# A transformer block on one core: gate and up columns split over the two banks of a couple

## The chip, the cores and the metric

The kernel runs on one core of one Trainium2 chip. The metric is the device time of one launch in microseconds (us), as the median of several runs; smaller is better. The engines are called here as the profile calls them: PE (TensorE, with PEld for its weight loads), DVE (VectorE), ACT (ScalarE), POOL (GpSimd) and SP (SyncE, which issues the DMAs).

## What is computed

One block with 2048 rows of 512 columns: a conditioned layer norm, attention with 32 query heads of 16 columns that share one key and one value head, and a gated feed-forward part of 1792 columns. What the change touches is the last one:

```python
h = _layernorm(x) * (1 + cb) + sb            # 2048 x 512
g = jnp.einsum("bsd,df->bsf", h, w_gate)     # 512 x 1792
u = jnp.einsum("bsd,df->bsf", h, w_up)       # 512 x 1792
h = _sigmoid(g) * u
out = jnp.einsum("bsf,fd->bsd", h, w_down)   # 1792 x 512
x = x + gb * out
```

## The kernel before

The 2048 rows are taken in 8 blocks of 256 rows (QU), each of two row tiles of 128 (t = 0, 1). Attention runs in 32 units (block, group of 8 heads) of 16 steps. A step has four tiles of scores `st` (ACT takes the exponent into `P`), four tiles `sa` of the unit two ahead, of which DVE takes the row maxima (`mx`), and the products of `P` and `V` into the bank `craw`. Every one of these tiles is 128 x 512 in one PSUM bank and is made by four matmuls of 64 rows by 32 columns of the array (the helper `columns`, line 141); two such row halves run side by side. `sa` has three banks, `st` two, `craw` one.

The feed-forward part of block b runs in pieces between the attention work of block b + 1, at most one piece after each half step (`piece`). It is cut in `Couple`s: two accumulation groups of 12 terms (four tiles of K times three products of high and low halves in fp16), each in its own bank `pgu` (tag "b", two banks). A couple runs 24 places; at each place the two row halves of the array work for different groups, and after 12 places they change over. At the end of a couple both groups' `end` is called, which issues what empties the two banks (the eviction). Which piece comes after which half step is set by a planner (`pick`, `pace`, `parts`) that knows the number of places, not their time. PE, DVE, ACT and SP keep the program's order; only the last part (block 7, "the tail", after the loop) is put in order by a scheduler.

Before the change, a couple of gate and up (`gu_group`, line 884) has 256 gate columns and the 256 up columns of the same place in one bank, row tile 0 in the first bank and row tile 1 in the second. Its eviction is, for the first bank, a tanh of the gate half and a copy of the up half, both on ACT, and for the second bank a copy of the up half on DVE and a tanh of the gate half on ACT. When both row tiles are done, `gated_rows` (POOL) multiplies them and two DMA transposes turn them (`turned`) for the product with `w_down`. There are seven such couples in a block, one for each 256 columns, and seven blocks in the loop: 49 evictions. In the tail, groups of columns (`gu_cols`, line 926) run with full 128 x 128 weights instead.

The gate and up weights are split into high and low halves once, by POOL, stored to DRAM (`wD`) and loaded again for each block. A tile `gw` holds all of K for 256 columns (1 MB), and there are two of them (GWB). At the beginning of a couple `ask` puts four loads of 256 KB for the next tile on a list, from which `drip` issues one at each half step behind the transposes; `fetched` issues what is left when a couple needs it.

Of the kernel before, what the change touches and what calls it, by code (L numbers as in the profile page):

```python
# [8 lines left out]
F16 = mybir.dt.float16  # L9
F32 = mybir.dt.float32  # L10
AF = mybir.ActivationFunctionType
# [5 lines left out]
P = 128  # L17
# [7 lines left out]
QU = 256  # L25
NQ = S // QU
NKB = S // P
NDC = D // P
# [3 lines left out]
SH = 4.0  # L32
SW = 16.0
# [51 lines left out]

PBUFS = 4
SBANKS = {"st": 2, "sa": 3}
GWB = 2
HBUFS = 18
ABUFS = 6  # L90
NCH = F // 256


@with_exitstack
def adaln_mqa_glu_kernel(
# [29 lines left out]
    dr = ctx.enter_context(tc.tile_pool(name="dr", bufs=1, space=DRAM))  # L125
# [69 lines left out]

    class Couple:
        def __init__(self, a, c):
            self.gs, self.stage, self.w, self.n = (a, c), a.stage, a.w, 2 * a.n

        def part(self, n0, n1):  # L200
            if n0 == 0:
                for g in self.gs:
                    g.open()
            m = self.gs[0].n
            for n in range(n0, n1):
                if n == m:
                    assert self.since is not None or done[0] > self.marks
                    take_over(self.since)
                for j in (1 - side[0], side[0]):
                    g = self.gs[j ^ (n >= m)]  # L210
                    l_, r_, *cut = g.term(n % m, slice(64 * j, 64 * j + 64))
                    columns(cut[0](g.bank) if cut else g.bank, l_, r_, n == 0, n == 2 * m - 1)
                if n == m - 1:
                    self.since, self.marks = None, done[0]
                    if open_[0]:
                        hand_over()
                        self.since = done[0]
            if n1 == self.n:
                for k, g in enumerate(self.gs):
                    g.end(g.bank, k == 1)  # L220
# [5 lines left out]
    def t32(name, shape=(P, 512)):  # L226
        return wp.tile(list(shape), F32, tag="f32", name=name, bufs=18)
# [27 lines left out]
    sp1 = Ordered(nc.sync)  # L255
# [74 lines left out]
    def split_weight(src, hi, lo, shape, then=None):  # L330
        w_ = t32("wst", [P] + shape)
        sp1.dma_start(w_, src)

        def split():
            pool.tensor_scalar(w_, w_, SW, 0.0, op0=ALU.mult, op1=ALU.add)  # L335
            pool.tensor_scalar(hi, w_, 1.0, 0.0, op0=ALU.mult, op1=ALU.add)
            pool.tensor_tensor(lo, w_, hi, op=ALU.subtract)
            if then is not None:
                defer(WSTORE, then)

        defer(WLATE, split)
# [417 lines left out]
        waits.append((now[0] + n, f_))  # L759

    WO = {}
    wD = dr.tile([NCH, P, NDC, 4, 256], F16, name="wD")
    CH = [*range(2, NCH), 0, 1]
    FS = [2 * c_ + e for c_ in CH for e in range(2)]

    def gw_tile():
        return P2.tile([P, NDC, 4, 256], F16, tag="gw", name="gw", bufs=GWB)

    def weight_jobs():
        jobs = []
        gw = {}

        def gate_up(c_, m, kk):
            if (m, kk) == (0, 0):
                gw[c_] = gw_tile()
            ks = slice(2 * kk, 2 * kk + 2)
            split_weight((w_gate, w_up)[m][2 * kk * P:2 * (kk + 1) * P, c_ * 256:(c_ + 1) * 256].rearrange("(k p) n -> p k n", p=P),
                         gw[c_][:, ks, m], gw[c_][:, ks, 2 + m], [2, 256],  # L780
                         (lambda: sp1.dma_start(wD[c_], gw.pop(c_))) if (m, kk) == (1, 1) else None)
# [3 lines left out]
        for c_ in CH:  # L785
            for m in range(2):
                for kk in range(2):
                    jobs.append(lambda c_=c_, m=m, kk=kk: gate_up(c_, m, kk))
# [9 lines left out]
    use, gws = [0], {}  # L798
# [9 lines left out]
    def fetched(upto):  # L808
        while loads and loads[0][0] <= upto:
            loads.pop(0)[1]()  # L810

    def ask(upto):
        while use[0] <= upto:
            k = use[0]
            gws[k] = gw = gw_tile()
            for z in range(NDC):
                loads.append((k, lambda gw=gw, k=k, z=z: sp1.dma_start(gw[:, z], wD[CH[k % NCH], :, z])))
            use[0] += 1

    def ffn_block(b, end_of_all=False):  # L820
        x1, xrs, h2, ups, ths, gT = {}, {}, {}, {}, {}, {}
        at = b * NCH
        HF = 6

        def wo_group(t):
# [55 lines left out]

            return t_, go

        def gu_group(c_, t):
            def begin():
                if t == 0:
                    fetched(at + c_)
                    ask(at + c_ + 1)
                    ths[c_], ups[c_] = t32("th"), t32("u")

            def term(n, rs):
                k, i = divmod(n, 3)
                gw = gws[at + c_]
                h_, w_ = ((0, 0), (1, 0), (0, 1))[i]
                return h2[t][0][rs, 4 * h_ + k, :], gw[rs, k, 2 * w_:2 * w_ + 2, :].rearrange("p m n -> p (m n)")

            def end(p_, second):
                ts = slice(256 * t, 256 * (t + 1))
                th, u_ = ths[c_], ups[c_]
                if second:  # L900
                    dve.tensor_copy(u_[:, ts], p_[:, 256:])
                    act.activation(th[:, ts], p_[:, :256], AF.Tanh, scale=0.5 / (SH * SW))
                else:
                    act.activation(th[:, ts], p_[:, :256], AF.Tanh, scale=0.5 / (SH * SW))
                    act.activation(u_[:, ts], p_[:, 256:], AF.Identity)
                if t == 1:
                    gated_rows(c_)

            return Group("gu", 12, "pgu", term, end, begin)

        def gated_rows(c_):
            th, u_ = ths.pop(c_), ups.pop(c_)
# [5 lines left out]
            gT[c_], go = turned(rows, f"g{c_}")  # L918
            if not tail:
                defer(GLATE, go)  # L920
                return
            go()
            while turns:
                drip()

        def gu_cols(c_, m):
            def begin():
                if m == 0:
                    ask(at + c_ + 1 if c_ < NCH - 1 else at + c_)
                    fetched(at + c_ + 1)  # L930

            def term(n, rs):
                e, (k, i) = n // 12, divmod(n % 12, 3)
                gw = gws[at + c_]
                h_, w_ = ((0, 0), (1, 0), (0, 1))[i]
                return gw[rs, k, 2 * w_ + m, e * P:(e + 1) * P], h2[k][rs, h_, :QU], lambda z: z[:, e * QU:(e + 1) * QU]

            def end(p_, second):
                if m == 0:
                    ths[c_] = th = t32("th")  # L940
                    act.activation(th, p_, AF.Tanh, scale=0.5 / (SH * SW))
# [4 lines left out]
                pool.tensor_tensor(g_[:, 1], th, g_[:, 0], op=ALU.subtract)  # L946
                gT[c_] = g_

            return Group("gu", 24, "pgu", term, end, begin)

        def g_of(h_, f, t, rs):
            c_, e = divmod(f, 2)
            if end_of_all:
                return gT[c_][rs, h_, e * QU + t * P:e * QU + (t + 1) * P]
            return gT[c_][rs, 4 * h_ + 2 * t + e, :]

        def down_group(t, lo):
            n_ = HF if lo == 0 else NFC - HF
# [37 lines left out]
        downs = [[down_group(t, lo) for t in range(2)] for lo in (0, HF)]  # L996
        if end_of_all:
            return wos, turn_rows, [[gu_cols(c_, m) for m in range(2)] for c_ in range(NCH)], downs
        gs = [Couple(gu_group(c_, 0), gu_group(c_, 1)) for c_ in range(NCH)]
        for g in gs:  # L1000
            g.needs = [(b, "h20"), (b, "h21")]
        for ds in downs:
            gs.append(Couple(*ds))
            gs[-1].needs = [(b, f"g{c_}") for c_ in (range(HF // 2) if len(gs) == NCH + 1 else range(NCH))]
        first = Couple(*wos)
        for g in [first, *gs]:
            g.b = b
# [249 lines left out]
```

## Time and profile before

| what | value |
|---|---|
| median of three runs | 1642.88 us (1642.43 to 1643.03) |
| the profiled execution: its own time | 1645.27 us |
| the profiled execution: span from first to last instruction | 1643.5 us, mean clock 0.991 |
| busy in the span | PE 1600.6, DVE 1415.8, ACT 1303.2, POOL 666.3 us |
| loop with feed-forward pieces | about 350 to 1550 us of the span |
| tail (block 7) | about 1553 to 1643 us |

The profiled execution is 2.39 us over the median. Busy time of PE is the union of its matmuls from start to modelled end, so that a wait shorter than the matmuls still in flight does not show as idle time; the timeline's starts show it. A row of the timeline gives the start in us, the length in us, the engine, the line, the operation and the tile, and how many were merged.

### The profile page before, as it was taken

How to read it: one execution, taken by the hardware profiler on the slowest of the kernel's cores; microseconds unless marked ns; L12 is line 12 of the kernel's file. 1: busy time of each engine (PE TensorE's matmuls, PEld its weight loads, DVE VectorE, ACT ScalarE, POOL GpSimd, SP SyncE). 2: the span in 40 equal slices, each digit the busy share in tenths (PEclk: the TensorE clock that was granted, in tenths of full speed). 3: DMA queues.
4: the chain of work that ended last, by engine and by line, in shares of the span. 5: the costliest groups of instructions: out<-in, count | busy, mean ns of one | idle time of the engine just before them, and what ended most of it. 6: DMA issues, size and time to landing. Idle time of an engine off the chain costs nothing.

```text
span 1643.5 us, 91921 instructions
## 1 busy us (share of the span) xinstructions
PE 1600.6 (97%) x41481; PEld 982.2 (60%) x41481; DVE 1415.8 (86%) x2400; ACT 1303.2 (79%) x2409; POOL 666.3 (41%) x827
## 2 busy tenths in 40 slices
PE   6899999999999999999999999999999999999998
PEld 3335444556666666666666566666666666665465
DVE  7789999999899999999999999999999999993041
ACT  5539989888888888888888888888888888888600
POOL 5453777244326232443226232543226322532222
PEclk9979999999999999999999999999999999999999
DMA  7121454136421433134412433134312432134522
GB/s 240 67 83 64 150 167 130 28 84 131 99 48 33 107 82 83 29 90 102 91 38 56 91 96 67 31 86 103 91 36 67 105 86 67 22 95 96 115 74 81
DMA packets 171301, 140.22 MB, mean 85 GB/s; under 512 B 96036, under 2 KB 129820, under 8 KB 170012
## 3 DMA queue, kind: packets, MB, share of 16 engines
q1 hardware_dynamic: 170908, 134.34, 32.0%
q8 instruction: 325, 5.32, 1.4%
q14 instruction: 68, 0.56, 0.1%
HBM read 97.18 MB, written 16.24 MB: 69 GB/s over the span
## 4 chain that ended last, share of the span: by engine, by line
PE 89%; DVE 3%; ACT 3%; DMA 2%; issue 1%; SPq 1%; POOL 0%; POOLq 0%; ACTq 0%
PE craw L141 25%; PE pgu L141 18%; PE sa L141 18%; PE st L141 11%; PE pd L141 8%; PE po L141 2%; PE pq L141 2%; PE pd L192 2%; PE pgu L192 2%; DVE mx L141 2%; ACT P L141 1%; DMA xall<-in_A_x_dram 1%; SPq L141 1%; ACT th L141 1%; DVE st L141 0%
## 5 line engine op out<-in xcount | busy, mean ns | idle before, releaser
L141 DVE TENSOR_REDUCE mx<-sa 128x1 f32<-128x512 f32 x2048 | 1309.7, 684 | 87.7 <-PE sa L141 38.5
L141 ACT ACTIVATE P<-st 128x512 f32<-128x512 f32 x2048 | 1180.7, 599 | 204.6 <-PE st L141 141.5
L141 PE MATMUL craw<-P,V 64*32 64x512 f32 x8192 | 1090.3, 597 | 2.0 <-issue 1.0
L141 PE MATMUL st<-qp,kp 64*32 64x512 f16 x8192 | 836.4, 379 | 6.4 <-ACT P L141 5.3
L141 PE MATMUL sa<-kp,qp 64*32 64x512 f16 (+1 forms) x7940 | 831.6, 378 | 7.1 <-DVE mx L141 5.5
L141 PEld LDWEIGHTS <-kp 64*32 64x32 f16 x8192 | 326.1, 91 | 262.6 <-issue 92.6
L141 PE MATMUL pgu<-gw,h 64*32 64x512 f16 x9408 | 422.2, 376 | 6.4 <-issue 3.6
L141 PEld LDWEIGHTS <-qp 64*32 64x32 f16 (+1 forms) x7940 | 269.5, 92 | 138.3 <-issue 52.2
L141 PEld LDWEIGHTS <-h 64*32 64x32 f16 (+1 forms) x9600 | 211.3, 92 | 90.5 <-issue 36.3
L141 PEld LDWEIGHTS craw<-P,V 64*32 64x32 f32 x8192 | 190.3, 105 | 24.7 <-issue 5.8
L141 PE MATMUL pd<-wdh,g 64*32 64x512 f16 x2688 | 136.6, 376 | 0.7
L913 POOL TENSOR_SCALAR th<-th 128x512 f32<-128x512 f32 x49 | 30.3, 618 | 242.2 <-ACT th L141 158.8
L565 POOL MEMSET qp<- 32x1024 f16 x60 | 56.6, 944 | 131.9 <-PE st L141 129.6
L141 PEld LDWEIGHTS <-g 64*32 64x32 f16 x4032 | 82.0, 92 | 30.8 <-issue 6.3
L721 POOL TENSOR_TENSOR raw<-raw 128x256 f32<-128x256 f32 x31 | 22.7, 732 | 164.7 <-DMA raw<-lD 142.3
L141 PE MATMUL pd<-wdl,g 64*32 64x512 f16 x1344 | 81.0, 376 | 0.0
L914 POOL TENSOR_TENSOR th<-th,u 128x512 f32<-128x512 f32 x49 | 62.8, 1282 | 4.1
L969 POOL TENSOR_TENSOR ot<-ot,gb 128x512 f32<-128x512 f32 x12 | 15.3, 1279 | 114.3 <-ACT ot L141 114.3
L917 POOL TENSOR_TENSOR gr<-th,gr 128x512 f16<-128x512 f32 x49 | 57.1, 1165 | 4.1
L141 PE MATMUL craw<-nought 64*32 64x1 f16 x357 | 58.2, 163 | 0.0
L141 PE MATMUL pq<-h,wdh 64*32 64x512 f16 (+1 forms) x688 | 54.8, 390 | 0.5 <-DVE h L141 0.4
L335 POOL TENSOR_SCALAR wst<-wst 128x512 f32<-128x512 f32 x46 | 28.4, 618 | 53.6 <-DMA wst<-in_B_w_down_dram 26.7
(156 smaller groups left out, 1131.3 us busy)
## 6 DMA issues: line engine op xcount, KB each, us to landing
gw<-wD SPq DMA_DIRECT2D x224, 256.0 KB
wD<-gw SPq DMA_DIRECT2D x7, 1024.0 KB
wm<-in_w_mod_dram SPq DMA_DIRECT2D x6, 1024.0 KB
qp<-qD SPq DMA_DIRECT2D x192, 32.0 KB
qD<-q SPq DMA_DIRECT2D x16, 256.0 KB
xr<-in_A_x_dram SPq DMA_DIRECT2D x16, 256.0 KB
out_dram<-ot SPq DMA_DIRECT2D x16, 256.0 KB
raw<-cs SPq DMA_DIRECT2D x248, 16.0 KB
```

Of the source, the lines that this page charges most:

```text
L141: return (lambda *a, **k: keep(f_(*a, **k))) if pinned else f_
L192: pe.matmul(cut[0](self.bank) if cut else self.bank, l_, r_, start=(n == 0), stop=(n == self.n - 1))
L335: pool.tensor_scalar(w_, w_, SW, 0.0, op0=ALU.mult, op1=ALU.add)
L565: eng.memset(qp[j:j + 32], 0.0)
L721: keep(pool.tensor_tensor(raw[:, :QU], raw[:, :QU], raw[:, QU:], op=ALU.mult))
L913: pool.tensor_scalar(th, th, 1.0, 1.0, op0=ALU.add, op1=ALU.mult)
L914: pool.tensor_tensor(th, th, u_, op=ALU.mult)
L917: pool.tensor_tensor(rows[:, 1], th, rows[:, 0], op=ALU.subtract)
L969: pool.tensor_tensor(ot, ot, mods[5], op=ALU.mult)
```

## The change

A couple now takes one row tile: 512 gate columns in one bank and the 512 up columns in the other (`gu_pair`). Three pairs of 512 columns and two row tiles make six couples; the remaining 256 columns stay as they were (`gu_last`), so that a block still has seven couples of the same number of places. The eviction of a pair is one tanh of 512 columns on ACT and one copy of 512 columns on DVE. The weights are kept by rows of K: a tile `gw` is [128, 4, 512] (512 KB: gate high, up high, gate low, up low for one tile of K), seven of them form the ring, and a block uses 14. A tile's slot is asked for again as soon as its last term in the second couple of a pair has been issued (`after`), in two loads of 256 KB; so a block still has 28 loads. The stores to DRAM are 28 of 256 KB with runs of 512 bytes for the pairs, in place of 7 of 1024 KB. The names of the turned tiles and the terms of the product with `w_down` follow.

```diff
-GWB = 2
+GWB = 7
+NPR = NCH // 2
+NGW = 4 * NPR + 2
...
-    wD = dr.tile([NCH, P, NDC, 4, 256], F16, name="wD")
+    wD = dr.tile([NPR, NDC, P, 4, 512], F16, name="wD")
+    wD1 = dr.tile([2, P, 2, 4, 256], F16, name="wD1")
...
+            def store():
+                for k in range(2):
+                    dst = wD[i // 2, 2 * kk + k, :, :, i % 2 * 256:(i % 2 + 1) * 256] if i < 2 * NPR else wD1[kk, :, k]
+                    sp1.dma_start(dst, g_[:, k])
...
+    def ask(spent):
+        while use[0] < min(spent + GWB, NGW * NQ):
...
+        def gu_pair(p, t, m):
+            def begin():
+                if m == 0:
+                    fetched(at + NDC * (p + 1) - 1)
+            def term(n, rs):
+                k, i = divmod(n, 3)
+                h_, w_ = ((0, 0), (1, 0), (0, 1))[i]
+                return h2[t][0][rs, 4 * h_ + k, :], gws[at + NDC * p + k][rs, 2 * w_ + m]
+            def end(p_, second):
+                if m == 0:
+                    ths[p, t] = th = t32("th")
+                    act.activation(th, p_, AF.Tanh, scale=0.5 / (SH * SW))
+                    return
+                u_ = t32("u")
+                dve.tensor_copy(u_, p_)
+                gated_rows(ths.pop((p, t)), u_, f"g{p}{t}")
...
-        gs = [Couple(gu_group(c_, 0), gu_group(c_, 1)) for c_ in range(NCH)]
+        gs = [Couple(gu_pair(p, t, 0), gu_pair(p, t, 1)) for p in range(NPR) for t in range(2)]
+        for p in range(NPR):
+            for k in range(NDC):
+                gs[2 * p + 1].after[12 + 3 * k + 2] = lambda spent=at + NDC * p + k + 1: ask(spent)
+        gs.append(Couple(gu_last(0), gu_last(1)))
```

The order of PE's instructions in the loop is the same, matmul for matmul, except for the names of the tiles and what the first matmul of a bank waits for. ACT's order at the first eviction (`th` and `u` are the eviction, `P` is attention), before:

```order
L141 ACTIVATE P_8815<-st 128x512
L141 ACTIVATE th<-pgu 128x256
L141 ACTIVATE u<-pgu 128x256
L141 ACTIVATE th<-pgu 128x256
L141 ACTIVATE P_8844<-st 128x512
```

and after:

```order
L143 ACTIVATE P_8836<-st 128x512
L143 ACTIVATE th<-pgu 128x512
L143 ACTIVATE P_8882<-st 128x512
L143 ACTIVATE cs<-craw 128x512
L143 ACTIVATE P_8900<-st 128x512
```

Three instructions stand between two exponents before, one of twice the width after. On DVE the copy keeps its place among the maxima and changes its width alone, 128x256 to 128x512. PE at the beginning of the second couple, where the two banks of the first are taken again (`h_...` are the turned rows of a row tile), before:

```order
L141 MATMUL st_8974<-qp_6718,kp_135 32x512
L141 LDWEIGHTS h20_7744 [waits DMAHW0_49,PE_49]
L141 MATMUL pgu_8983<-gw_8428,h20_7744 32x512 [waits Activation_49]
...
L141 LDWEIGHTS h21_7839
L141 MATMUL pgu_8984<-gw_8428,h21_7839 32x512 [waits Activation_49]
```

and after:

```order
L143 MATMUL st_9012<-qp_6747,kp_135 32x512
L143 LDWEIGHTS h21_7874 [waits DMAHW3_49]
L143 MATMUL pgu_9018<-gw_7774,h21_7874 32x512 [waits Activation_49]
...
L143 LDWEIGHTS h21_7874
L143 MATMUL pgu_9019<-gw_7774,h21_7874 32x512 [waits DVE_49]
```

Before, both banks wait for ACT; after, the first waits for ACT and the second for DVE. In the tail, PE between the last use of the first `gw` slot that is loaded again and the first use of its new content, before (28 matmuls between the two):

```order
L192 MATMUL pgu_50416<-h2c_50381,gw_49676 128x256
...
L192 LDWEIGHTS gw_50445 [waits DMAHW4_49]
L192 MATMUL pgu_50511<-h2c_50367,gw_50445 128x256
...
L192 LDWEIGHTS gw_50445 [waits DMAHW5_49]
```

and after (37 between the two):

```order
L194 MATMUL pgu_50477<-h2c_50377,gw_48869 128x256
...
L194 LDWEIGHTS gw_50506 [waits DMAHW7_49]
L194 MATMUL pgu_50518<-h2c_50391,gw_50506 128x256
...
L194 LDWEIGHTS gw_50506 [waits DMAHW0_49]
```

The scheduler has put more matmuls between release and use than stood there before.

More of the change, by code (lines that the diff above doesn't have):

```diff
@@ L197, in __init__ @@
         def __init__(self, a, c):
-            self.gs, self.stage, self.w, self.n = (a, c), a.stage, a.w, 2 * a.n
+            self.gs, self.stage, self.w, self.n, self.after = (a, c), a.stage, a.w, 2 * a.n, {}
         def part(self, n0, n1):
@@ L217, in part @@
                         self.since = done[0]
+                if n in self.after:
+                    self.after[n]()
             if n1 == self.n:
@@ L810, in fetched, with weights @@
             loads.pop(0)[1]()
[L812 to L817, printed above, removed]
-            use[0] += 1
+    def ask(spent):
+        while use[0] < min(spent + GWB, NGW * NQ):
+            u = use[0]
+            gws[u] = gw = gw_tile()
+            i = u % NGW
+            src = wD[i // NDC, i % NDC] if i < NDC * NPR else wD1[i - NDC * NPR].rearrange("p k m n -> p (k m n)").rearrange("p (m n) -> p m n", n=512)
+            for z in range(2):
+                loads.append((u, lambda gw=gw, src=src, z=z: sp1.dma_start(gw[:, 2 * z:2 * z + 2], src[:, 2 * z:2 * z + 2])))
+            use[0] += 1
+    def weights(b, i, k, w_, m):
+        at = b * NGW
+        if i < 2 * NPR:
+            return gws[at + NDC * (i // 2) + k][:, 2 * w_ + m, i % 2 * 256:(i % 2 + 1) * 256]
+        return gws[at + NDC * NPR + k // 2].rearrange("p m n -> p (m n)").rearrange("p (k m n) -> p k m n", k=2, m=4)[:, k % 2, 2 * w_ + m]
     def ffn_block(b, end_of_all=False):
         x1, xrs, h2, ups, ths, gT = {}, {}, {}, {}, {}, {}
-        at = b * NCH
+        at = b * NGW
         HF = 6
```

63 lines of the change are left out of this document (34 added, 29 removed).

## The prediction

> **What bounds the kernel now.** I read the page first (busy time by engine), then the table by stages for the loop, then the groups of instructions, then the list of waits, and at last the timeline around single evictions.
>
> ```profile
> PE 1600.6 (97%) x41481; PEld 982.2 (60%) x41481; DVE 1415.8 (86%) x2400; ACT 1303.2 (79%) x2409; POOL 666.3 (41%) x827
> 500.00:700.00 200.00, 198.53 (x5890) 131.78 (x5882) 189.42 (x318) 172.91 (x321) 82.11 (x97) 1.00 0.29 69
> ```
>
> The second row is a stretch of the loop; after the bounds and the length come PE, PEld, DVE, ACT and POOL busy, the granted clock, the DMA share and GB/s. PE is busy for 99% of it at full clock, DVE for 95%, ACT for 86%. So PE's order sets the pace, DVE follows closely, and the 1% of idle PE looks as if nothing could be won at the banks. The list of waits says the same: for the banks of gate and up that ACT empties it has 0.6 us, for the `sa` banks that DVE empties 5.5 us.
>
> ```profile
> PE sa L141 <- DVE mx L141: 5.5, 13, 1.4
> ...
> PE pgu L141 <- ACT u L141: 0.6, 4, 0.2
> ```
>
> But PE counts as busy while earlier matmuls are in flight, so a wait under 0.4 us doesn't show there. The timeline's starts show it. An eviction of gate and up in the middle of the loop:
>
> ```profile
> 791.57 0.43 PE L141 MATMUL st<-qp,kp 64*32 64x512 f16 x4
> ...
> 791.78 0.68 PE L141 MATMUL pgu<-gw,h 64*32 64x512 f16 x16
> 792.22 0.42 PE L141 MATMUL sa<-kp,qp 64*32 64x512 f16 x4
> ...
> 792.68 0.38 ACT L141 ACTIVATE th<-pgu 128x256 f32<-128x256 f32 x1
> ...
> 792.74 0.41 DVE L141 COPY u<-pgu 128x256 f32<-128x256 f32 x1
> 792.86 0.43 PE L141 MATMUL st<-qp,kp 64*32 64x512 f16 x4
> 792.94 0.39 ACT L141 ACTIVATE u<-pgu 128x256 f32<-128x256 f32 x1
> ...
> 793.21 0.41 ACT L141 ACTIVATE th<-pgu 128x256 f32<-128x256 f32 x1
> 793.39 0.89 PE L141 MATMUL pgu<-gw,h 64*32 64x512 f16 x16
> ...
> 793.90 0.39 PE L141 MATMUL sa<-kp,qp 64*32 64x512 f16 x4
> ```
>
> Undisturbed, a piece starts 0.21 us after the last `st` (791.57 to 791.78), and 16 of its matmuls take 0.44 us (791.78 to 792.22). The first piece of the next couple starts 0.53 us after the `st` (792.86 to 793.39) and takes 0.51 us (to 793.90). That is 0.32 + 0.07 = 0.39 us lost. The releases explain both parts. The first bank is free when ACT's `u` ends at 793.33, and PE starts 0.06 later. The second is free when ACT's second `th` ends at 793.62, which holds the other row half.
>
> **The change part by part.**
>
> Evictions. The kernel has a close likeness of the new form already: a couple of the product with `w_down` ends with one 512-wide instruction on ACT and one on DVE.
>
> ```profile
> 530.23 0.59 ACT L141 ACTIVATE ot<-pd 128x512 f32<-128x512 f32 x1
> ...
> 530.28 0.68 DVE L141 TENSOR_TENSOR ot<-pd,gb 128x512 f32<-128x512 f32 x1
> 530.41 0.41 PE L141 MATMUL st<-qp,kp 64*32 64x512 f16 x4
> ...
> 530.87 0.76 PE L141 MATMUL pgu<-gw,h 64*32 64x512 f16 x16
> 530.88 1.88 DVE L141 TENSOR_REDUCE mx<-sa 128x1 f32<-128x512 f32 x3
> ...
> 531.30 0.40 PE L141 MATMUL sa<-kp,qp 64*32 64x512 f16 x4
> ...
> 531.73 0.40 PE L141 MATMUL sa<-kp,qp 64*32 64x512 f16 x4
> ```
>
> There the piece starts 0.46 us after the `st` and takes 0.43 us, so 0.25 us is lost, all at the first bank. The durations of the new instructions:
>
> ```profile
> L941 ACT ACTIVATE th<-pgu 128x512 f32<-128x512 f32 x7 | 4.2, 597 | 37.4 <-PE pgu L192 29.0 <-POOL gc L946 4.7 <-DMA gw<-wD 3.6
> L141 ACT ACTIVATE th<-pgu 128x256 f32<-128x256 f32 x98 | 38.4, 392 | 0.1
> L141 DVE COPY u<-pgu 128x256 f32<-128x256 f32 x49 | 20.4, 416 | 34.2 <-PE pgu L141 34.0
> L141 DVE TENSOR_TENSOR ot<-pd,gb 128x512 f32<-128x512 f32 x12 | 8.2, 681 | 0.0
> L141 DVE TENSOR_REDUCE mx<-sa 128x1 f32<-128x512 f32 x2048 | 1309.7, 684 | 87.7 <-PE sa L141 38.5 <-PE st L141 22.9 <-PE pgu L141 0.9
> ```
>
> A tanh of 512 columns is in the tail at 597 ns. A copy of 512 columns is not in the trace; both other 512-wide reads of a bank by DVE take 681 to 684 ns, so I take 683, which is 267 more than the 416 of now. In the eviction above, `th` would run from 792.68 to 793.28, and PE would start at 793.33 or 793.34 rather than 793.39. The copy would run from 792.74 to 793.42; the second bank's first matmuls are due about 0.11 us after the first's, at 793.44. The 0.07 us in the piece goes, and 0.05 to 0.07 us at its start. So 0.12 to 0.14 us per eviction; the likeness says 0.39 - 0.25 = 0.14, and I take that.
>
> About a third of the evictions (14 of the 45 that I went through in the timeline between 340 and 1490 us) have a hand-over of the bank `craw` just ahead of the piece:
>
> ```profile
> 777.08 0.40 PE L141 MATMUL st<-qp,kp 64*32 64x512 f16 x4
> ...
> 777.60 0.89 PE L141 MATMUL pgu<-gw,h 64*32 64x512 f16 x16
> ...
> 778.31 0.40 PE L141 MATMUL sa<-kp,qp 64*32 64x512 f16 x4
> ```
>
> The piece comes 0.52 us after the `st` and takes 0.71 us. The likeness with a hand-over:
>
> ```profile
> 713.04 0.40 PE L141 MATMUL st<-qp,kp 64*32 64x512 f16 x4
> ...
> 713.52 0.70 PE L141 MATMUL pgu<-gw,h 64*32 64x512 f16 x16
> ...
> 714.04 0.37 PE L141 MATMUL sa<-kp,qp 64*32 64x512 f16 x1
> ```
>
> 0.48 and 0.52 us: 0.04 + 0.19 = 0.23 us less. Six of seven evictions in a block change form, 42 in all; a third of them is 14. The term is 28 x 0.14 + 14 x 0.23 = 3.9 + 3.2 = 7.1 us. Its bounds: 42 x 0.05 = 2.1 us, if only the earlier end of ACT counts and DVE's longer copy takes up the rest, and 28 x 0.39 + 14 x (0.31 + 0.28) = 19 us, if every wait went (0.31 and 0.28 are 0.52 - 0.21 and 0.71 - 0.43).
>
> The Trainium skill (Perfetto Trace Analysis, section Optimizing Scalar/DVE Operations) says that where Scalar and Vector aren't saturated but cause bubbles elsewhere, breaking up instructions may let work finish sooner; that speaks for the old form, and by it the evictions would gain nothing. Here the parts run one after the other on one engine and a bank is free after its last part alone, so I go by the row.
>
> DVE's extra work is 42 x 0.267 = 11.2 us in all. It delays the maxima, and so the release of `sa` banks, which PE would wait for. Cover: `sa` has three banks. In the likeness DVE's eviction is as long as the new one, and the next `sa` still come 0.43 us apart (531.30, 531.73), the undisturbed spacing. I take 0 and keep up to 3 us (a quarter not absorbed). ACT is freed of 3 x 392 - 597 = 579 ns in each eviction; the exponents behind it come earlier, which I count as nothing since PE is then past the wait.
>
> Loads and SP. As many loads of the same size; tiles are asked for in the second half of a couple and used at the earliest 9 places into the next, and a couple lasts some 6 steps (12 half steps of over 1.2 us). Landing takes about 3.2 us (below). SP now waits for PE's last use of a slot inside a couple, 14 times a block rather than 7, and behind it stand the DMAs `qp<-mh` that `st` needs.
>
> ```profile
> SPq L141 <- PE pgu L141: 1.7, 1, 1.7
> L141 PE MATMUL st<-qp,kp 64*32 64x512 f16 x8192 | 836.4, 379 | 6.4 <-ACT P L141 5.3 <-DMA qp<-mh 0.3 <-issue 0.2
> ```
>
> PE waits 0.3 us in all for those DMAs, and SP once for a slot: nothing, at most 1 us. The 21 extra stores come while the weights are split, ahead of the loop:
>
> ```profile
> 809.54 2.22 SPq L141 DMA_DIRECT2D gw<-wD  x4
> 100.00:350.00 250.00, 243.55 (x5625) 120.65 (x5628) 238.32 (x405) 214.46 (x393) 153.06 (x193) 0.97 0.35 108
> ```
>
> An issue costs SP 2.22 / 4 = 0.56 us, so 12 us more on SP, with the DMA engines 35% busy. Nobody waits for a store before the first load. I take 0; at worst the issues hit the `qp<-mh` of the four units there, 2 us. POOL's work is the same.
>
> Tail. Its end is set by PE, which waits twice for loads:
>
> ```profile
> 1590.09 21.43 SPq L817 DMA_DIRECT2D gw<-wD  x20
> 1582.45 10.66 PE L192 MATMUL pgu<-h2c,gw 128*128 128x256 f16 x96
> 1593.29 0.83 PE L192 MATMUL pgu<-h2c,gw 128*128 128x256 f16 x6 [0.18 <-DMA gw<-wD]
> 1594.49 15.25 PE L192 MATMUL pgu<-h2c,gw 128*128 128x256 f16 x138 [0.37 <-DMA gw<-wD]
> ```
>
> From issue (1590.09) to use (1593.29) are 3.2 us. A matmul there takes 10.66 / 96 = 0.11 us; the order now has 37 of them between release and use, 4.1 us, in place of 28. The 0.18 + 0.37 = 0.55 us go: -0.5 us. The bounds are -0.6 and, if both of the slots that are filled late (one for each pair) were uncovered, 2 x 3.2 = +6 us.
>
> Sum: -7.1 - 0.5 = -7.6 us against the execution's own 1645.27, so 1637.7; that execution was 2.4 us over the median of 1642.88, which gives **1635.3 us** by the median.
>
> **The rivals.**
> A change within 0.2% (about 3.3 us, the least that a measurement of this kernel can tell from none) is called the same.
>
> *The wait moves to DVE.* The second bank now waits for DVE, whose queue is 95% full. If the copy began 0.3 us later than ACT's tanh rather than 0.06, it would end at 793.66, later than the second `th` does now, and the loss of 0.07 would stay or grow. Then only the start's 0.05 us is won, 2.1 us, and the tail: 1640.3. Against it: in both evictions shown DVE starts 0.05 to 0.06 us behind ACT.
>
> *DVE becomes the bound.* If DVE has no slack between evictions, the 11.2 us come on top and what PE wins at its bank it waits out at `sa`: 1642.9 + 11.2 = 1654.1. It decides against the change once 29 of the 42 longer copies (29 x 0.267 = 7.7 us) aren't absorbed. For it: 95% busy. Against: the idle 87.7 us before its maxima, and the spacing in the likeness. The Trainium skill (Perfetto Trace Analysis, section Identifying the Most-Contended Engine) takes occupancy as a fair measure for Vector and Scalar and not for TensorE; by that rule DVE is the contended engine here, and loading it is a loss.
>
> *The relief goes further.* The exponents behind an eviction come earlier too and the waits go altogether: up to 19 us, as bounded above. The middle between 7 and 19, with the tail's 0.5, is 13.5 us: 1629.4.
>
> **How the numbers follow.** Forecast 0.60, wait moves 0.20, DVE the bound 0.08, more relief 0.12. The forecast's own range is 1632 to 1640 (its term between the ACT part with a little more, and 11 us). For 8 in 10 I go a little past the middle of the case with more relief below, 1628, and above to the case that moves the wait with 3 us of loss on DVE or SP, 1644. Faster by over 0.2%: 0.60 x 0.9 + 0.12 + 0.2 x 0.2 = 0.70; slower 0.07; the same 0.23.
>
> **What would show it.** Right: groups of 42 `th` 128x512 on ACT near 597 ns and 42 copies 128x512 on DVE near 683; from the last `st` to the first `pgu` about 0.46 us, and the piece behind it 0.43 us; PE's busy time some 7 us lower. Wrong: that piece still at 0.5 us with a late DVE copy (the first rival); PE idle for `mx` well over the present 5.5 us, or DVE without idle time (the second); PE waiting for `gw` in the loop or the tail.

## The result and the profile after

The changed kernel takes 1628.7 us (median of six runs, 1628.2 to 1636.3) beside 1642.7 us for the kernel before (six runs, 1640.0 to 1647.5): the ratio is 0.992, 95% interval 0.990 to 0.994. A second measurement gave 1633.5 beside 1647.2 us, ratio 0.993 (0.990 to 0.995). Runs of one kernel differ by several us, so kernels of different measurements are compared below by their ratios to the kernel before. The profiled execution of the changed kernel took 1629.06 us, its span is 1627.3 us.

Busy time of the engines, and the stretch of the loop from 500 to 700 us:

```profile
PE 1585.3 (97%) x41481; PEld 987.3 (61%) x41481; DVE 1417.1 (87%) x2400; ACT 1288.7 (79%) x2325; POOL 666.2 (41%) x827
500.00:700.00 200.00, 199.65 (x6001) 133.80 (x5990) 192.54 (x323) 173.96 (x313) 86.12 (x104) 1.00 0.27 71
```

The same 41481 matmuls keep PE busy 15.3 us less. In the same 200 us PE now does 6001 of them, not 5890, 1.9% more, though its busy share in that stretch rose by only 0.6%. DVE is busy only 1.3 us more in all, since its maxima take 9.9 us less; ACT is busy 14.5 us less.

An eviction of a pair in the middle of the loop (start, length, engine, line, operation):

```profile
785.75 0.59 ACT L143 ACTIVATE th<-pgu 128x512 f32<-128x512 f32 x1
...
785.81 0.68 DVE L143 COPY u<-pgu 128x512 f32<-128x512 f32 x1
785.94 0.42 PE L143 MATMUL st<-qp,kp 64*32 64x512 f16 x4
...
786.39 0.76 PE L143 MATMUL pgu<-gw,h 64*32 64x512 f16 x16
...
786.83 0.40 PE L143 MATMUL sa<-kp,qp 64*32 64x512 f16 x4
...
787.04 0.40 PE L143 MATMUL st<-qp,kp 64*32 64x512 f16 x4
```

ACT and DVE start 0.06 us apart. The piece starts 0.45 us after the last `st` (before 0.53) and takes 0.44 us (before 0.51), and behind it `sa` and `st` are 0.21 us apart again. With a hand-over of `craw` ahead of the piece:

```profile
769.04 0.40 PE L143 MATMUL st<-qp,kp 64*32 64x512 f16 x4
...
769.53 0.76 PE L143 MATMUL pgu<-gw,h 64*32 64x512 f16 x16
...
770.10 0.40 PE L143 MATMUL sa<-kp,qp 64*32 64x512 f16 x4
```

0.49 us to the piece and 0.57 us for it, rather than 0.52 and 0.71. At this one place nothing came of it: the half step lasts 1.87 us in both kernels (776.65 to 778.52 before, 768.45 to 770.32 after), because the `st` ahead of the piece starts 0.16 us later in it than before. Single evictions thus gain mostly between 0 and 0.6 us; what counts below is their sum. The groups of instructions:

```profile
L143 ACT ACTIVATE th<-pgu 128x512 f32<-128x512 f32 x42 | 24.9, 594 | 0.1
L143 DVE COPY u<-pgu 128x512 f32<-128x512 f32 x42 | 28.6, 682 | 21.6 <-PE pgu L143 21.6
L143 DVE TENSOR_REDUCE mx<-sa 128x1 f32<-128x512 f32 x2048 | 1299.8, 683 | 69.6 <-PE sa L143 33.2 <-PE st L143 12.6 <-PE craw L143 0.3
```

The two new instructions take 594 and 682 ns; 597 and 683 were forecast. DVE's idle time ahead of its maxima fell from 87.7 to 69.6 us. The waits of PE that matter below, by the list of waits (total, times, longest):

```profile
PE sa L143 <- DVE mx L143: 6.2, 15, 1.4
...
PE sa L143 <- issue: 1.6, 1, 1.6
...
PE pgu L143 <- DMA gw<-wD: 1.2, 2, 0.9
PE pgu L143 <- issue: 1.1, 2, 0.9
PE craw L143 <- issue: 1.1, 1, 1.1
...
PE st L143 <- DMA qp<-mh: 0.9, 2, 0.5
```

Last, the tail, where PE runs its gate and up matmuls without a wait:

```profile
1566.78 23.09 PE L194 MATMUL pgu<-h2c,gw 128*128 128x256 f16 x210
```

**Where the time went, by the starts.** Around an eviction (from 1 us ahead of the first `th` to 2.5 us behind it) I took how far PE's starts fall behind the undisturbed pace (16 matmuls in 0.43 us). Over the 42 evictions that changed form the changed kernel loses 10.3 us less, 0.245 us each; over the 7 that did not, 0.01 us in all. The sum depends a little on how it is cut: the three half steps from each of the 42 evictions on are 11.0 us shorter. The last `st` of the loop comes 15.7 us sooner (1551.2 and 1535.5 us), of which 2.1 us were there at the first piece (350.8 and 348.7 us); the tail gives 0.5. So of 13.6 us in the loop some 3 us are not at the evictions.

### The profile page after: what moved, and what is told of

It reads as the page before. It is cut to its first block, busy times and chain, and to the rows that moved or that the text cites. A ratio compares the mean times of both kernels' runs of the same rounds, so it can differ in the third digit from the quotient of the medians.

```text
span 1627.3 us, 91846 instructions
## 1 busy us (share of the span) xinstructions
PE 1585.3 (97%) x41481; PEld 987.3 (61%) x41481; DVE 1417.1 (87%) x2400; ACT 1288.7 (79%) x2325; POOL 666.2 (41%) x827
## 3 DMA queue, kind: packets, MB, share of 16 engines
q8 instruction: 325, 5.32, 1.3%
## 4 chain that ended last, share of the span: by engine, by line
PE 88%; DVE 4%; ACT 2%; DMA 2%; POOL 1%; issue 1%; SPq 1%; POOLq 0%; ACTq 0%; DVEq 0%
PE craw L143 24%; PE sa L143 18%; PE pgu L143 17%; PE st L143 11%; PE pd L143 8%; PE po L143 2%; PE pgu L194 2%; PE pq L143 2%; PE pd L194 2%; DVE mx L143 2%; ACT th L143 1%; DMA lc<-lD 1%; SPq L143 1%; DMA xall<-in_A_x_dram 1%; ACT P L143 1%
## 5 line engine op out<-in xcount | busy, mean ns | idle before, releaser
L143 DVE TENSOR_REDUCE mx<-sa 128x1 f32<-128x512 f32 x2048 | 1299.8, 683 | 69.6 <-PE sa L143 33.2
L143 PE MATMUL pgu<-gw,h 64*32 64x512 f16 x9408 | 407.4, 376 | 3.2 <-DMA gw<-wD 1.2
L143 PEld LDWEIGHTS craw<-P,V 64*32 64x32 f32 x8192 | 184.4, 105 | 21.7 <-issue 2.6
L143 DVE COPY u<-pgu 128x512 f32<-128x512 f32 (+1 forms) x49 | 31.6, 644 | 34.9 <-PE pgu L143 34.8
```

The source lines that it names most:

```text
L143: return (lambda *a, **k: keep(f_(*a, **k))) if pinned else f_
```

## The experiments

The theories that the runs were to part: *A*, everything is the form of the eviction; *B*, the form gives the 10.3 us that the starts show, and the new ring and its loads the rest; *C*, the ring and the loads carry it.

**New layout, old form of eviction.**

```diff
-                    act.activation(th, p_, AF.Tanh, scale=0.5 / (SH * SW))
+                    for z in range(2):
+                        act.activation(th[:, 256 * z:256 * z + 256], p_[:, 256 * z:256 * z + 256], AF.Tanh, scale=0.5 / (SH * SW))
...
-                dve.tensor_copy(u_, p_)
+                dve.tensor_copy(u_[:, :256], p_[:, :256])
+                act.activation(u_[:, 256:], p_[:, 256:], AF.Identity)
```

> The changed kernel, but the eviction of a pair is cut as before: ACT empties the first bank by two tanh of 256 columns, DVE copies 256 columns of the second and ACT the other 256. Couples, weights in DRAM, ring and loads stay new. Theory A, all that the loop won (13.5 us) is the form of the eviction: 1628.7 + 13.5 = 1642.2 us. Theory B, the form is worth what the starts around the 42 evictions show (10.3 us) and the other 3 us come from the new ring and its loads: 1639.0 us. Rival C, the ring and the loads carry it: 1629 us.

1641.3 us beside 1645.3 us; ratio 0.998 (0.996 to 1.000). Against the changed kernel's 0.992 and 0.993 that is 9 to 10 us, and at the 42 evictions its starts fall 11.2 us further behind. As a ratio A said 0.9997, B 0.998 and C 0.992: B fits, C is out, and A lies at the edge of the interval.

**Old layout, new form of eviction.**

```diff
                 th, u_ = ths[c_], ups[c_]
                 if second:
-                    dve.tensor_copy(u_[:, ts], p_[:, 256:])
-                    act.activation(th[:, ts], p_[:, :256], AF.Tanh, scale=0.5 / (SH * SW))
+                    dve.tensor_copy(u_, p_)
                 else:
-                    act.activation(th[:, ts], p_[:, :256], AF.Tanh, scale=0.5 / (SH * SW))
-                    act.activation(u_[:, ts], p_[:, 256:], AF.Identity)
+                    act.activation(th, p_, AF.Tanh, scale=0.5 / (SH * SW))
```

> The kernel before with its old couples, tiles and ring, but all 49 evictions are one 512-wide tanh on ACT for the first bank and one 512-wide copy on DVE for the second. (The up half of row tile 0 thus gets a tanh and the gate half of row tile 1 gets none: for the time alone.) Theory A: 49 evictions at 13.5 / 42 = 0.32 us each: 1642.7 - 15.7 = 1627.0 us (the tail's 0.5 us is not in it). Theory B: 49 at 10.3 / 42 = 0.245 us: 1642.7 - 12.0 = 1630.7 us. Rival C: 1642 us.

1637.6 us, ratio 0.995 (0.993 to 0.997): 8 us faster, less than A (0.990) or B (0.993) said. At the evictions it does the same as the changed kernel: the 42 differ by 0.65 us in sum, and the 7 others gain 1.0 us. What is missing lies elsewhere. Its list of waits, rows of PE that end in "issue" (PE waited for nothing that the profile shows):

```profile
PE pgu L141 <- issue: 5.1, 7, 1.1
...
PE st L141 <- issue: 2.1, 4, 1.1
...
PE craw L141 <- issue: 1.5, 3, 0.8
```

The kernel before had

```profile
PE pgu L141 <- issue: 3.6, 6, 0.8
...
PE sa L141 <- issue: 1.0, 2, 0.5
PE craw L141 <- issue: 1.0, 3, 0.5
```

That is 8.7 and 5.6 us in the two kernels with the old layout, against 3.8 us in the changed kernel's three rows (4.9 us when it was measured again). One of these places in the kernel before:

```profile
719.30 0.37 PE L141 MATMUL pgu<-gw,h 64*32 64x512 f16 x1
...
720.49 0.61 PE L141 MATMUL pgu<-gw,h 64*32 64x512 f16 x10 [0.82 <-issue]
```

PE stops for 1.2 us in the middle of a piece, with no semaphore to wait for. The DMA queues have one of kind "instruction":

```profile
q8 instruction: 325, 5.32, 1.4%
```

325 packets in 5.32 MB, 16 KB each, one every 4.2 us in the loop (median). They follow PE's program: PE starts some 250 matmuls and weight loads between two packets, and it has 2 x 41481 of them in all, 255 for each packet. At the stop above such a packet starts at 718.28, ends at 719.20, and PE resumes 1.29 us behind its end. I then went through all half steps that last over 0.45 us longer than the same half step does in the median of nine executions (before, after, after measured again and six of the variants here), and called those *late instructions* in which the instruction that ends the stop waits for no semaphore and comes 1.2 to 1.7 us behind the end of such a packet. The span is not picked to fit: in the kernel before all 14 stops of over 0.45 us in the loop without a semaphore end 1.29 to 1.62 us behind a packet, while 1.2 to 1.7 us behind a packet is 11% of the time. The rest are mostly waits for small transfers (`qp<-mh`, `lc`) or `gw`, or what follows them. Each row is one profiled execution:

| kernel | late instructions: half steps, us | other long half steps: number, us |
|---|---|---|
| before | 12, 9.5 | 2, 1.1 |
| old layout, new form | 13, 12.4 | 4, 3.0 |
| after | 3, 3.7 | 6, 4.6 |
| after, measured again | 4, 4.6 | 10, 9.9 |
| new layout, old form | 3, 2.3 | 5, 9.0 |
| copy on ACT (below) | 3, 1.8 | 9, 7.5 |
| loads at every second half step (below) | 2, 1.8 | 1, 0.7 |
| the same, old form (below) | 1, 0.5 | 3, 2.5 |
| the same, half of each bank read (below) | 1, 0.5 | 3, 2.0 |

The new layout thus has some 5 to 7 us less of late instructions than the kernel before, and 3.5 to 9 us more of the others. That its net is small and varies (4 us in the run with the old form) is these two against each other. The long half steps are not mere chance: six of the nine of the changed kernel are long again in its second measurement.

**More work on DVE, and the copy on ACT.** Two edits of the changed kernel:

```diff
 dve.tensor_copy(u_, p_)
+xm = wp.tile([P, 1], F32, tag="xm", name="xm", bufs=2)
+dve.tensor_reduce(xm, u_, axis=AX.X, op=ALU.max)
```

> The changed kernel, and behind each of the 42 copies DVE takes a maximum over the 512 columns of the copy in SBUF, which holds no bank and which nobody uses: some 42 x 0.6 to 0.68 = 25 to 29 us more work on DVE. Theory: DVE has slack between evictions and PE hardly waits for it; 0 to 5 us, 1629 to 1634 us. Rival, DVE is at its bound after the change: all of it shows, 1654 to 1658 us.

```diff
-dve.tensor_copy(u_, p_)
+act.activation(u_, p_, AF.Identity)
```

> The changed kernel, but ACT makes the copy of the second bank too, behind its tanh; DVE has no part in the eviction (27 us less work on it), ACT as much work as before the change and a little more. Theory, the time from the couple's last matmul to the release of the later bank sets the loss: the second bank comes free some 0.45 us later than with DVE (0.54 + 0.54 behind each other, against 0.68), so 42 x 0.45 = 19 us slower, 1647 us. Rival, fewer instructions or a lighter DVE made the gain: 1629 us or less.

The extra maxima take 28.8 us of DVE (42 x 686 ns), and the kernel takes 1645.0 us, ratio 1.000 (0.999 to 1.001): 12 to 13 us more than the changed kernel, by the starts 12.8 us at the evictions, 0.31 us each. Neither side had it: a little under half shows. One place:

```profile
1471.58 0.69 DVE L143 TENSOR_REDUCE xm<-u 128x1 f32<-128x512 f32 x1
...
1472.03 0.38 PE L143 MATMUL sa<-kp,qp 64*32 64x512 f16 x1
...
1472.92 0.40 PE L143 MATMUL sa<-kp,qp 64*32 64x512 f16 x4
```

The second `sa` comes 0.89 us after the first, where the changed kernel has 0.43; PE waits there for the maxima that stand behind `xm`.

With the copy on ACT: 1645.2 us, ratio 1.000 (0.998 to 1.001), 12 to 13 us more than the changed kernel, by the starts 16.6 us (0.39 each; 0.45 was expected). DVE is relieved by 28.6 us and it doesn't help:

```profile
1471.50 0.59 ACT L143 ACTIVATE th<-pgu 128x512 f32<-128x512 f32 x1
...
1471.98 0.60 ACT L143 ACTIVATE u<-pgu 128x512 f32<-128x512 f32 x1
...
1472.14 1.10 PE L143 MATMUL pgu<-gw,h 64*32 64x512 f16 x16
...
1473.07 0.40 PE L143 MATMUL sa<-kp,qp 64*32 64x512 f16 x4
```

The piece takes 0.93 us (1472.14 to 1473.07), since its second bank is ACT's until 1472.58. Two 512-wide reads in a row on one engine cost more than the old four of 256 on two (16.6 against 11.2 us by the starts, in the same layout). So it isn't the number of instructions that counts, and a lighter DVE doesn't make up for a later release of the second bank.

**The pace of the loads.** The changed kernel again, and the same edit on the new and on the old layout:

```diff
         elif loads:
-            loads.pop(0)[1]()
+            paced[0] += 1
+            if paced[0] % 2:
+                loads.pop(0)[1]()
```

> The changed kernel once more, beside the three that follow, on one chip. Expected: the ratio to the kernel before found first (0.992, 0.990 to 0.994), some 1631 us if the kernel before takes 1645. The profile tells whether the late instructions of TensorE (idle time with 'issue' as its end, and no semaphore) stand at the same places and stay at some 7 us in the loop, against 15 to 16 us in the two kernels with the old layout.

> The changed kernel with its weight loads issued at every second half step only, rather than at each, so that a burst of eight loads lasts twice as long at half the rate; nothing else differs. Theory, TensorE's late instructions come where loads crowd the DMA engines: fewer of them, 2 to 4 us less time than the changed kernel beside it. Rival, they stand at fixed dense places of TensorE's program whatever the loads do: the same time. Against both: the longer stretch of loads meets more of these places, up to 5 us more.

> The kernel before (old couples, old ring, old eviction) with its loads issued at every second half step only. Theory, the bursts of four loads, one in each half step behind a couple's beginning, make TensorE's instructions late: of the 21 late stretches of the kernel before (14.6 us) half or more go, 5 to 8 us less, 1638 us if the kernel before takes 1645. Rival, the late stretches hang on the place in TensorE's program alone and the new layout won by other means: no change.

The new layout with loads at every second half step takes 1620.9 us (1619.6 to 1623.2), ratio 0.985 (0.982 to 0.987), 12.6 us less than the changed kernel beside it (1633.5): far more than was expected, and the fastest kernel here that computes the whole block. The evictions are the same (0.6 us in sum). In the table above, late instructions fall from 4.6 to 1.8 us and the other long half steps from 9.9 to 0.7 us, together 12.0 (the two profiled executions are 14.7 us apart). So most of it is not what the theory spoke of, but the waits for small transfers. The edit thins out the loads in the program's order; in time SP issues them in runs either way. In the changed kernel measured again 129 of the 203 loads that follow another in the loop come within 0.9 us of it, in the spread kernel 79 of 206. PE's wait for `qp<-mh` there:

```profile
PE st L143 <- DMA qp<-mh: 3.1, 4, 0.9
```

In the spread kernel that row is gone from the list. One of these waits, and what SP issued ahead of it:

```profile
770.11 0.40 PE L143 MATMUL st<-qp,kp 64*32 64x512 f16 x4 [0.92 <-DMA qp<-mh]
```

```profile
740.38 1.00 SPq L143 DMA_DIRECT2D gw<-wD  x2
...
742.98 0.85 SPq L143 DMA_DIRECT2D gw<-wD  x2
...
748.00 1.80 SPq L143 DMA_DIRECT2D gw<-wD  x4
...
755.10 0.69 SPq L143 DMA_DIRECT2D raw<-lD  x1
...
765.96 2.93 SPq L143 DMA_DIRECT2D qp<-mh  x4
```

The half step of this wait starts at 767.50. In the spread kernel the same half step starts at 763.36, and SP has:

```profile
736.37 0.53 SPq L143 DMA_DIRECT2D gw<-wD  x1
...
737.43 0.42 SPq L143 DMA_DIRECT2D gw<-wD  x1
...
741.94 1.67 SPq L143 DMA_DIRECT2D gw<-wD  x2
...
746.78 0.69 SPq L143 DMA_DIRECT2D raw<-lD  x1
...
758.34 2.96 SPq L143 DMA_DIRECT2D qp<-mh  x4
```

In the 16 us ahead of `raw<-lD` (128 KB) eight loads are issued in the changed kernel, four in the spread one. So it goes out 12.4 rather than 16.6 us ahead of the half step. Between it and `qp<-mh` (2 KB each) SP's queue holds two transposes of gated rows, which POOL makes behind its work on `raw`; so the last `qp<-mh` is issued 1.4 us behind the start of the half step (765.96 + 2.93) rather than 2.1 us ahead of it. The same place in five units: with four loads there (both kernels of the old layout at the full pace, and the spread kernel in its new and its old form) SP is done with `qp<-mh` 1.2 to 2.6 us ahead each time; with seven or eight (the new layout at the full pace: the changed kernel twice, the old form, the copy on ACT) from 0.9 us ahead to 3.7 us behind. So these delays go back to the loads in SP's queue, and they are the price of the new layout's bursts of eight. DVE's wait for the small load `lc`, changed kernel again and then spread:

```profile
DVE rc L143 <- DMA lc<-lD: 13.1, 9, 6.3
```

```profile
DVE rc L143 <- DMA lc<-lD: 8.7, 2, 8.0
```

Without the longest of each list, 6.8 us in eight waits became 0.7 in one. At some of these PE waits in turn for the maxima behind `rc` (0.70 us at 928.61 in the changed kernel measured again).

The old layout with the same pace takes 1661.2 us, ratio 1.010 (1.006 to 1.013), 14 us *more*; the theory said 5 to 8 less. It has a new first row in PE's list:

```profile
PE pgu L141 <- DMA gw<-wD: 16.9, 13, 3.2
```

A ring of two tiles leaves one couple's time for a tile's four loads, and at half the pace they come late. What the theory spoke of did happen: stops of over 0.33 us with no semaphore and a packet of instructions 1.2 to 1.7 us before their end were 21 in the kernel before (14.6 us, a part of which is normal spacing) and are 5 (3.9 us) here. So at half the pace the late instructions fall in both layouts; in the old one PE's own stops for `gw` may have had a part in it. The new layout can afford the slower pace (one wait of 1.4 us for `gw` in its list), the old one can't. No run changed the depth of the ring alone.

Smaller grains in place of a slower pace, in the changed kernel:

```diff
-            for z in range(2):
-                loads.append((u, lambda gw=gw, src=src, z=z: sp1.dma_start(gw[:, 2 * z:2 * z + 2], src[:, 2 * z:2 * z + 2])))
+            for z in range(4):
+                rs, ms = slice(z % 2 * 64, z % 2 * 64 + 64), slice(z // 2 * 2, z // 2 * 2 + 2)
+                loads.append((u, lambda gw=gw, src=src, rs=rs, ms=ms: sp1.dma_start(gw[rs, ms], src[rs, ms])))
```

> The changed kernel with each weight load of 256 KB cut in two of 128 KB (by partitions, runs of the same length), one at each half step: the same average rate as the kernel with loads at every second half step (1620.9 us, ratio 0.985), in finer grains. Theory, what is late are the small transfers and instruction blocks that stand behind a load: half the load, half the delay, 1617 to 1619 us. Rival, only the average rate counts: 1621 us. Against both: SP issues twice as many loads (0.4 to 0.56 us each) ahead of the same small transfers: 1623 to 1627 us.

1648.8 us, ratio 1.002 (1.000 to 1.004): 28 us slower than the spread kernel, far beyond what any theory said. No row with "issue" is left in PE's list, but there is this:

```profile
PE po L143 <- POOL a L726: 15.8, 6, 4.6
PE st L143 <- DMA qp<-mh: 9.5, 8, 2.7
```

```profile
444.60 5.76 SPq L143 DMA_DIRECT2D gw<-wD  x8
450.46 3.08 SPq L143 DMA_DIRECT2D qp<-mh  x4
```

SP needs 5.76 / 8 = 0.72 us for one issue here, twice as many of them stand in its queue, and the small transfers (`qp<-mh` above) come behind. The third case of the expectation was right in kind, with a price several times too small. At the place of five units shown above, seven or eight loads stand ahead of `raw<-lD` again, and the last `qp<-mh` goes out 0.3 us ahead of the half step to 2.9 us behind its start. How much of the 28 us is SP's queue and how much the DMA engines no run parts.

**What is left at an eviction.** Three edits of the spread kernel: the old form (as above), a maximum over 160 columns behind the copy (`u_[:, :160]`, 320 ns each), and an eviction that reads half of each bank:

```diff
-                    act.activation(th, p_, AF.Tanh, scale=0.5 / (SH * SW))
+                    pool.memset(th[:, 256:], 0.0)
+                    act.activation(th[:, :256], p_[:, :256], AF.Tanh, scale=0.5 / (SH * SW))
...
-                dve.tensor_copy(u_, p_)
+                pool.memset(u_[:, 256:], 0.0)
+                dve.tensor_copy(u_[:, :256], p_[:, :256])
```

> The kernel with loads at every second half step (new layout, 1620.9 us), with the eviction of a pair cut as before the change (two tanh of 256 columns; a copy of 256 on DVE and of 256 on ACT). It prices the form of the eviction where little else disturbs. Theory, 10.3 to 11.2 us as the starts around the evictions showed: 1631 to 1632 us, ratio 0.991. Rival, the 7.1 us of the forecast: 1628 us, ratio 0.989.

> The kernel with loads at every second half step, and behind each of the 42 copies DVE takes a maximum over 160 columns of the copy, some 0.3 us, 13 us in all (the run with 512 columns, 0.686 us each, cost 0.31 us each). Theory, DVE has a slack of about 0.37 us at an eviction and work beyond it shows in full: 0 to 1 us, 1621 to 1622 us. Rival, there is no such threshold and 45% of any extra work shows: 6 us, 1627 us.

> The kernel with loads at every second half step, but the eviction of a pair reads only the first 256 columns of each bank (POOL fills the rest of th and u with zeros): half of gate and up is left out. Theory, the time to a bank's release still sets the loss, and ACT's tanh ends 0.2 us sooner (0.39 rather than 0.59): 42 x 0.2 = 8 us, 1612 to 1613 us. Rival, what is left at an eviction has another cause: 1621 us.

The old form takes 1631.7 us, ratio 0.991 (0.989 to 0.993): 10.8 us more than the spread kernel, 11.0 by the starts. This is the cleanest price of the form. Half a bank takes 1613.6 us, ratio 0.980 (0.978 to 0.982): 7.3 us less by the medians and by the starts, 0.17 us at each eviction for 0.2 us less of ACT, as the theory said. But DVE's copy is 0.27 us shorter there too, and at the price of DVE's work in the next run that could be a good part of it; the run doesn't part the two. The 13.4 us of extra maxima cost 7.3 us by the medians, of which 4.3 us stand at the evictions: there is no slack of 0.37 us, and the rival was right.

**More time for the eviction.** In the changed kernel the planner leaves the half step behind a couple's end empty:

```diff
-            sizes += places(g.n // 2, hb + len(sizes), rate, most, 3 if g.stage == "q" and leg == 0 else None, g.w)
+            sizes += places(g.n // 2, hb + len(sizes), rate, most, (3 if g.stage == "q" else 1) if leg == 0 else None, g.w)
```

> The changed kernel, but the planner leaves the half step behind a couple's end empty, so that the next couple's first piece comes one half step (some 1.2 us) later, and spreads its matmuls over the others. Theory, what is left of the loss at a bank (0.22 to 0.35 us at each of 42 evictions, 0.42 to 0.56 at the 7 others: some 15 us) goes, less what the denser pieces cost: 8 to 15 us faster than the changed kernel, about 1618 us. Rival, the denser pieces (24 matmuls in place of 16 in a quarter of the half steps) make ACT and DVE wait and the instructions late: the same time or slower, 1629 to 1635 us.

1649.5 us, ratio 1.002 (1.001 to 1.004), 16 us slower than the changed kernel: worse than the rival said too. The first row of PE's waits is now

```profile
PE st L143 <- ACT P L143: 25.1, 68, 1.1
```

against 6.1 us before this edit. In a half step without a piece PE comes to its next `st` before ACT has taken the exponents of the last two (0.6 us each). The pieces are also what gives ACT its time, so here leaving one out gave the eviction no room.

## Why the prediction came out as it did

Forecast: 7.6 us off the execution, 1635.3 us, range 1628 to 1644. Measured: 14.0 us off, 1628.7 us. The direction and the mechanism at the banks were right; the term for the evictions was too small, and the one for the loads, put at nothing, was not nothing. That the time lies inside the range, 0.7 us above its lower end, is in part luck: some 10.8 of the 14 us are in terms that the forecast had.

- *Evictions, 7.1 us: measured 10.3 by the starts, 10.8 by the run that took the form back where little else disturbs.* The lengths of the new instructions, the 0.45 us to the piece and its 0.44 us (forecast 0.46 and 0.43) were right, and so, on average, was 0.23 us for an eviction with a hand-over (0.239). What failed is the step "0.39 - 0.25 = 0.14" for a plain one; it measured 0.247 us. It counted the way to the piece and the piece alone. In the old form the `sa` and `st` behind the piece, which starts at 793.90, still stood 0.25, 0.22 and 0.27 us apart rather than 0.21 to 0.22: a further 0.09 us, which the new form also saves.

```profile
794.15 0.40 PE L141 MATMUL st<-qp,kp 64*32 64x512 f16 x4
...
794.37 0.40 PE L141 MATMUL sa<-kp,qp 64*32 64x512 f16 x4
...
794.64 0.40 PE L141 MATMUL st<-qp,kp 64*32 64x512 f16 x4
```

- *DVE's 11.2 us of extra work, taken as 0.* The net of the form is a gain in each run, so the forecast stands, but not its reason. The extra maxima cost 0.10 to 0.17 us for 0.32 us and 0.31 us for 0.69 us at an eviction: about a third to a half of such work shows. The third `sa` bank is not the full cover that the likeness made it; what the copy itself lost there isn't parted from the gain by any run. The Trainium skill (Perfetto Trace Analysis, section Identifying the Most-Contended Engine) takes occupancy as a fair measure for Vector; at 95% it was a fair warning for further work, though not for this change.
- *Loads and SP, "nothing, at most 1 us".* That step was wrong in kind. It named SP's queue and the `qp<-mh` in it, but priced them by the waits of the kernel before, where four loads stand ahead of `raw<-lD` and not eight. It didn't ask what else uses the DMA engines: the rows with "issue" in the list of waits of before (3.6 us for `pgu` alone) were left unread. The new layout took some 5.8 us of late instructions away and gave 3.5 us back, mostly in late small transfers, in the profiled pair; the run with the old form puts the layout's net at 4 us with the tail's 0.5 in it. PE's waiting for `gw` in the loop, one of the signs of being wrong, did appear, but at 1.2 us in two places.
- *Tail, -0.5 us.* Both waits for `gw` are gone, and the tail is 0.5 us shorter.
- *The rivals.* The wait did not move to DVE: the copy began 0.06 us behind the tanh, and the second bank was free at 786.49, when PE's first matmuls for it were due (0.11 us behind 786.39). DVE did not become the bound. "The relief goes further" (1629.4 us) named the time that came, for a reason that is only half of it. Breaking up instructions (the Trainium skill, Perfetto Trace Analysis, section Optimizing Scalar/DVE Operations, says that it may let work finish sooner) did not help here: the two runs with the old form are some 10 us slower with the smaller instructions. But in them ACT has three of the four parts, one behind the other, and a bank comes free with its last part; two parts on each engine were not run, so the runs don't part the number of instructions from their share between the engines.

In the profiled pair the terms are: evictions -10.3, late instructions -5.8, other long half steps +3.5, tail -0.5, and -2.1 that was there at the first piece, which sum to -15.2 of the 16.2 us between the spans; 1.0 us is not assigned.

Open: why the new layout has fewer late instructions at the same pace of one load for each half step. Its loads come in fewer, longer bursts (eight behind every second couple, rather than four behind each), and in the kernel before all 21 stops come within 7 us of the issue of a load, which is 43% of the loop's time. That the number of bursts counts would fit this, but no run changed it alone. That a late block of instructions is the cause of those stops is inferred from the fixed 1.2 to 1.7 us behind its packet and from the pace of the loads; the trace has no releaser for them.

## What to carry to other kernels

Two accumulators that are needed together were emptied fastest here by one instruction each, side by side on two engines. What that is worth is read at the starts of PE's matmuls through the half step behind, not in its idle time. When weights are streamed beside a full PE, look at the "issue" rows, at waits for tiny transfers, and at how many loads stand ahead of these in the issuing engine's queue. With a ring deep enough, fewer loads in a row were worth 12.6 us here, nearly as much as the change itself; the same bytes in twice as many loads were not. An edit of one engine's work is best priced in the kernel with the fewest chance stops.

## What was not expected of the hardware

- PE's instructions come in packets of 16 KB over the DMA engines (325 of them, 255 matmuls and weight loads for each). PE has stops of 0.4 to 2 us without a semaphore, from which it resumes 1.2 to 1.7 us behind a packet's end. With one 256 KB load behind each half step of the program these cost 9.5 to 12.4 us in the old layout and 1.8 to 4.6 us in the new one, and 0.5 to 1.8 us in the new one with a load at every second half step.
- SP's queue carried a delay on: with eight loads in place of four ahead of it, one transfer (`raw<-lD`) went out 1.5 to 4.3 us later at the same place of five units (changed kernel measured again against spread), and the transposes and small transfers behind it came later too.
- One issue on SP took 0.72 us in a row of eight 128 KB loads; one such load at each half step made the kernel 28 us slower than one of 256 KB at every second.
- Work of 0.32 and 0.69 us added to a DVE that is 95% busy showed by a third to a half, though DVE had 69.6 us of idle time ahead of its maxima.
